# Linear attention with balanced routing on one core: order of copies, lists and first products where attention ends

## The chip, the cores and the metric

One core of a Trainium2 chip. The metric is the device time of one execution in microseconds (us), the median of three runs. The profiled execution is one more run; all starts and durations below come from it, counted from the start of its span.

## What is computed

The reference has two blocks. The first is a linear attention with decay (RWKV-5): for each of 4 batches and 8 heads a state of 48 x 48 goes through 768 steps. The second routes its output, 3072 tokens of 384 values, to 8 experts of 384 tokens each, greedily by the highest logits.

```python
for t in range(S):
    cur = einsum('bhd,bhe->bhde', u * k[:, :, t], v[:, :, t])
    y[:, :, t] = einsum('bhd,bhde->bhe', r[:, :, t], state + cur)
    state = w * state + einsum('bhd,bhe->bhde', k[:, :, t], v[:, :, t])
x = y.transpose(0, 2, 1, 3).reshape(B * S, H * D)
logits = x @ w_gate                      # 3072 x 8
for idx in argsort(-logits.flatten()):   # highest first
    tok, e = idx // E, idx % E           # skipped if tok is taken or e has its 384
for e in range(E):
    out[mask_e] = relu(x[mask_e] @ w1[e]) @ w2[e]     # 384 -> 1024 -> 384
```

Everything is fp32.

## The kernel before

**Attention** (class `Mild`). The work is cut into 24 units n of 128 tokens, four batches for each of six chunks of the sequence. For a unit, TensorE turns r and k, makes the pairs of r and k (`pairs`, g_ps L504), which VectorE masks into AT (L508); ScalarE writes AT's diagonal (L495) from a sum that GpSimd (rk L442 and L443) and VectorE (dd L448) prepare; `outputs` (L531) accumulates the state's part and AT's part in y_ps (L542), and ScalarE copies it to x (L560). Rows of x are turned (`rows_turned`, x_ps L591), copied (xr L598) and stored to DRAM (L599, issued by SyncE). After each fourth unit the router's logits of a chunk are made: `gate` (lg_ps L571, copy L576) and `logits`, one transpose (lt_ps L581) and one copy into LG (L582). The order of `run` is written out by hand, under a manual schedule: an engine executes its instructions in the order of the calls. In a unit in which a chunk ends (`full`, n = 4, 8, 12, 16, 20), `outputs` with its copy of x comes first and `logits` of the chunk before after it.

**Routing** (class `Assignment`). A search on VectorE raises or lowers thresholds until each expert's tokens are chosen. It uses TensorE for counts (prop against ind, L944; wide against ones_h, L955), running sums (st_ps L1075) and lists (some_ps L1408, list_ps L1426). `early` is a generator that already works while attention still runs, on the first five chunks: it picks one expert, the star, and a first list of 256 of its tokens (e_some_ps L1199, then list_ps). The list `steps` says at which places of attention's units its parts are called: its entries name a unit, counted from the end, and a place in it ("states" lies between the state's products and AT's in `outputs`, "last" after `outputs`, "rows" by the rows of units 20 and 21).

**Experts** (class `Experts`). `gather` (xg L1513) issues one indirect DMA per 128 rows from GpSimd; `load_weights` has SyncE load w1 and w2 (L1506), once the expert's number is known (L1499). `turned` turns 128 rows (xT_ps L1528) and ScalarE copies them to xT (L1529). `hidden` multiplies by w1 (h_ps L1541), 3 products for each of 8 outputs j of 128 features, and ScalarE applies relu (L1543). An fp32 product is two matmul instructions.

The first list is worked off by `Experts.early` (L1697), a generator that yields after every product, so that `go(m)` can put m pieces between the steps of the search: two blocks of 128 rows are turned (e_xT_ps L1705, each block in a PSUM tile of its own) and copied (L1706), then 8 outputs of 3 products of 256 columns (e_h_ps L1711, relu L1714), then the second layer (e_o_ps L1719), copied (L1723) and scattered (L1637). At the end of attention the order is written out by hand: the rows of unit 22 out, both blocks of the first list, the rows of unit 23 out, two products, then the search for the first full expert (expert n = 1 of the loop) with products between its steps. Its rows are gathered and `turned`, with the second search's first steps before and between, and the rest of the first list's products ahead of the first turn. From then on `Experts.run` takes over, with `hidden` of n = 1 first; a scheduler, no longer the order of the calls, places the later searches' instructions by their costs. For n = 1 the variable `late` in `run` is true.

PSUM tiles with the same tag (y_ps, kT_ps, rT_ps, g_ps) share space. y_ps takes two banks of 512 fp32 values.

Of the kernel before, what the change touches and what calls it, by code (L numbers as in the profile page):

```python
# [10 lines left out]
F32 = mybir.dt.float32  # L11
# [4 lines left out]
AF = mybir.ActivationFunctionType  # L16
# [258 lines left out]
class Mild:  # L275
# [252 lines left out]
            else:  # L528
                nc.vector.tensor_mul(S, kv, wc)

    def outputs(self, n, between=None):  # L531
        nc, HP, D, C = self.nc, self.HP, self.D, self.C
        b, c = self.units[n]
        AT, rT = self.live[n]["AT"], self.live[n]["rT"]
        vt, S0 = self.vts[:, n % self.NV], self.states[:, b]
        y_ps = self.ps.tile([128, 2, 512], F32, name="y_ps")
        yv = y_ps[:, :, 0:2 * T].rearrange("p o (i t) -> p o i t", t=T)
        seen = set()

        def add(h, lhsT, rhs, stop):  # L540
            o, q = h // 2, h % 2
            nc.tensor.matmul(yv[q * PD:(q + 1) * PD, o // 2, o % 2, :], lhsT, rhs, start=(o // 2, q) not in seen,  # L542
                             stop=stop, skip_group_check=True)
            seen.add((o // 2, q))

        if c > 0:
            for i in range(HP // 2):
                for a in (i, i + HP // 2):
                    for z in range(2):
                        rows = slice(z * PD, z * PD + D)  # L550
                        add(self.head(a, z), S0[rows, a, :], rT[rows, a, :], False)
        if c > 0:
            self.keep(n)
        if between is not None:
            between()
        for a in range(HP):
            for z in range(2):
                add(self.head(a, z), vt[:, self.head(a, z), :], AT[:, z, a, :], True)
        xT = self.xpool.tile([128, HP, T], F32, name=f"x{n % 5}")
        nc.scalar.copy(xT.rearrange("p (o i) t -> p o i t", i=2), yv)  # L560
        self.xts[n] = xT
        del self.live[n]
# [18 lines left out]
        nc.tensor.transpose(lt_ps, lg, self.ident)  # L581
        nc.scalar.copy(self.LG[:, c * B:(c + 1) * B, :], lt_ps.rearrange("p (b e) -> p b e", b=B)[:, :, 0:self.E])  # L582

    def rows_turned(self, ns, tag):
        nc, HP = self.nc, self.HP
        shape = [128, len(ns), HP, T]
        ps = (self.walk.ps if tag == "few" else self.ps).tile(shape, F32, name="x_ps", tag=tag)
        P = PD + self.D
        for i, n in enumerate(ns):
            for o in range(HP):  # L590
                nc.tensor.transpose(ps[:, i, o, 0:P], self.xts[n][0:P, o, :], self.ident[0:P, 0:P])  # L591
        return ps

    def rows_out(self, ns, ps):
# [18 lines left out]
    def run(self, step):  # L613
# [38 lines left out]
        for n in range(N):  # L652
# [47 lines left out]
                if n + 2 < N:  # L700
                    self.diagonal(n + 2, halves[1])
            if n == N - 1:
                self.rows((N - 4, N - 3), "g_ps")
                step(n, "rows")
            self.outputs(n, lambda: step(n, "states"))
            if split:
                self.diagonal(n + 2, halves[1])
            if full:
                self.logits(n // B - 1)
            if n == N - 4:  # L710
                self.own_sum(N - 1)
            step(n, "last")
# [736 lines left out]
def rwkv5_eagle_then_base_layer_balanced(  # L1449
# [12 lines left out]
    nc = tc.nc  # L1462
# [21 lines left out]
    class Experts:  # L1484
# [48 lines left out]
            *_, xT = self.turned(ahead, lambda c: self.ps_t.tile([128, KD, 128], F32, name="xT_ps"))  # L1533
            return xT

        def hidden(self, w1, xT, m, half, progress):
            hid = self.h.tile([128, KF, CAP], F32, name="hid")
            for j in range(KF):
                h_ps = self.ps_h.tile([128, CAP], F32, name="h_ps")
                for f in range(KD):  # L1540
                    nc.tensor.matmul(h_ps[:, 0:m], w1[:, f, ts(j, 128)], xT[:, f, 0:m],  # L1541
                                     start=(f == 0), stop=(f == KD - 1))
                nc.scalar.activation(hid[:, j, 0:m], h_ps[:, 0:m], AF.Relu)  # L1543
                if j == KF // 2 - 1:
                    half(hid)
                progress((j + 1) / KF)
            return hid

        BLOCKS = dict(h0=(0, 0), h1=(0, 1), h2=(1, 0), h3=(1, 1), h4=(2, 0), h5=(2, 1))
# [102 lines left out]
        def run(self, ahead, later, rows, pulls={}, xT=None):  # L1652
            xT, lead = xT or self.turn(ahead), True
            while ahead:
# [28 lines left out]
                def at_product(part):  # L1683
                    progress(1 + part)

                hid = self.hidden(w1, xT, nb * 128, half if whole else lambda hid: None, progress)
                if whole:
                    self.sums_of(left, self.HID_SUMS if many else self.SEVEN_LATE)
                    (self.fifteen if many else self.seven)(left, right, tok, rows, at_product)
# [7 lines left out]
        def early(self, ps, pool, w1, w2, xg, tok, rows, have):  # L1697
            NE = tok.shape[1]
            m = NE * 128
            xT = self.turns[0].tile([128, KD, CAP], F32, name="xT")  # L1700
            hid = pool.tile([128, KF, m], F32, name="e_hid")
            for c in range(NE):
                xT_ps = ps.tile([128, KD, 128], F32, name="e_xT_ps", tag=("y_ps", "rT_ps")[c % 2])
                for f in range(KD):
                    nc.tensor.transpose(xT_ps[:, f, :], xg[:, c, ts(f, 128)], ident)  # L1705
                nc.scalar.copy(xT[:, :, ts(c, 128)], xT_ps)  # L1706
                yield
            for j in range(KF):
                h_ps = ps.tile([128, m], F32, name="e_h_ps", tag=("kT_ps", "rT_ps")[j % 2])
                for f in range(KD):  # L1710
                    nc.tensor.matmul(h_ps, w1[:, f, ts(j, 128)], xT[:, f, 0:m], start=(f == 0), stop=(f == KD - 1))  # L1711
                    if f < KD - 1:
                        yield
                nc.scalar.activation(hid[:, j, :], h_ps, AF.Relu)  # L1714
                yield
            for c in range(NE):
                o_ps = ps.tile([128, DX], F32, name="e_o_ps", tag=("y_ps", "g_ps")[c % 2])
                for j in range(KF):
                    nc.tensor.matmul(o_ps, hid[:, j, ts(c, 128)], w2[:, j, :], start=(j == 0), stop=(j == KF - 1))  # L1719
                    if j < KF - 1:  # L1720
                        yield
                o_sb = pool.tile([128, DX], F32, name="e_o_sb", bufs=2)
                nc.scalar.copy(o_sb, o_ps)  # L1723
                self.scatter(o_sb, have["to"][:, c:c + 1], next(rows))
                yield

    with ExitStack() as whole:
# [6 lines left out]
        with ExitStack() as part:  # L1734
# [7 lines left out]
            def on_tokens(tok):  # L1742
# [2 lines left out]
            early = walk.early(on_star, on_tokens)  # L1745
            U = mild.N
            steps = [(U - 7, "first"), (U - 7, "paired"), (U - 6, "paired"), (U - 5, "products"), (U - 5, "paired"),
                     (U - 3, "turning"), (U - 3, "turning"), (U - 3, "paired"), (U - 2, "last"),
                     (U - 1, "rows"), (U - 1, "last")]

            def step(n, at):
# [3 lines left out]
            with tc.manual_schedule():  # L1755
# [4 lines left out]
                def go(m):  # L1760
                    for _ in range(m):
                        next(pieces, None)

                mild.rows_out((U - 2,), one)
                go(NE)
                mild.rows_out((U - 1,), last)
                go(2)
                search = walk.likely_steps(**first, on_fmax=lambda fmax: have.update(v=x.load_weights(1, fmax)))
                for m in (2, 5, 2, 5, 2, 6, 5):
                    next(search)  # L1770
                    go(m)
                next(search, None)
# [10 lines left out]
                ahead = 1, xg, to, *have["v"]  # L1783
                turned = x.turned(ahead, lambda c: mild.ps.tile([128, KD, 128], F32, name="xT_ps",
                                                                tag=("kT_ps", "rT_ps")[c % 2]))
                go(8)
                next(search)
                go(2)
                next(search)
                for m in (0, 0, 99):  # L1790
                    go(m)
                    xT = next(turned)
                walk.book(first, first=True)
# [86 lines left out]
```

## Time and profile before

| | |
|---|---|
| median of 3 runs | 398.09 us (398.03 to 398.3) |
| profiled execution | 397.39 us |
| its span | 395.7 us |
| instructions | 8692, of them 3243 matmuls |
| attention's last output copied (unit 23) | about 125.3 us from the span's start |
| first product of the first list | 129.6 us |
| first product of the first full expert | 155.09 us |

The span runs from the first to the last instruction that the profile records; 1.7 us of the execution lie outside it. A row of the timeline has the start, the busy time, the engine, the line, the operation, output and inputs by name, sizes, and in brackets the engine's idle time just before with what ended it. PE is TensorE's matmuls, PEld its weight loads, DVE is VectorE, ACT is ScalarE, POOL is GpSimd and SP is SyncE. A row may merge several instructions (x and their number).

### The profile page before, as it was taken

How to read it: one execution, taken by the hardware profiler on the slowest of the kernel's cores; microseconds unless marked ns; L12 is line 12 of the kernel's file. 1: busy time of each engine (PE TensorE's matmuls, PEld its weight loads, DVE VectorE, ACT ScalarE, POOL GpSimd, SP SyncE). 2: the span in 40 equal slices, each digit the busy share in tenths (PEclk: the TensorE clock that was granted, in tenths of full speed). 3: DMA queues.
4: the chain of work that ended last, by engine and by line, in shares of the span. 5: the costliest groups of instructions: out<-in, count | busy, mean ns of one | idle time of the engine just before them, and what ended most of it. 6: DMA issues, size and time to landing. Idle time of an engine off the chain costs nothing. (4 is left out here: it accounts for less than half of the span.)

```text
span 395.7 us, 8692 instructions
## 1 busy us (share of the span) xinstructions
PE 381.1 (96%) x3243; PEld 289.3 (73%) x3243; DVE 266.9 (67%) x934; ACT 162.0 (41%) x429; POOL 138.4 (35%) x173
## 2 busy tenths in 40 slices
PE   7899999999999999999999999999999999999993
PEld 5678888888877765587578569558757856966991
DVE  6755777576885677897839819979578663952630
ACT  4998888888873312222222122121222222222130
POOL 7888877666732013032121120302303211040020
PEclk9999999999999999999999999999999999999998
DMA  9999999898692155371460650109209173380010
GB/s 120 156 183 200 200 173 205 156 169 157 117 342 81 42 200 217 96 282 42 160 239 16 214 210 2 60 0 333 87 21 354 59 275 131 92 308 2 2 61 27
DMA packets 95331, 57.29 MB, mean 145 GB/s; under 512 B 77232, under 2 KB 89520, under 8 KB 95280
## 3 DMA queue, kind: packets, MB, share of 16 engines
q1 hardware_dynamic: 91936, 47.21, 47.7%
q0 software_dynamic: 3104, 9.44, 6.8%
q8 instruction: 27, 0.44, 0.5%
q14 instruction: 24, 0.20, 0.2%
q10 hardware_dynamic: 240, 0.00, 0.0%
HBM read 47.20 MB, written 9.44 MB: 143 GB/s over the span
## 5 line engine op out<-in xcount | busy, mean ns | idle before, releaser
L1541 PE MATMUL h_ps<-xT,w 128*128 128x384 f32 (+1 forms) x384 | 120.7, 467 | 0.6 <-ACT xT L1529 0.6
L1541 PEld LDWEIGHTS h_ps<-xT,w 128*128 128x128 f32 x384 | 66.4, 190 | 38.1 <-issue 2.5
L1543 ACT ACTIVATE hid<-h_ps 128x384 f32<-128x384 f32 (+1 forms) x64 | 29.7, 465 | 91.1 <-PE h_ps L1541 85.1
L495 ACT ACTIVATE AT<-ident,dd 128x128 f32<-128x128 f32 x192 | 59.6, 391 | 1.9 <-DVE dd L448 1.8
L1513 POOL DMA_INDIRECT xg<-x_rows,tok x22 | 22.4, 1017 | 95.6 <-PE h_ps L1541 32.1
L1637 POOL DMA_INDIRECT out_dram<-o_all,to x16 | 17.9, 1120 | 94.6 <-DVE o_all L1625 62.2
L508 DVE COPY_PREDICATED AT<-mask,g_ps 128x512 f32<-128x512 uint8 x48 | 32.6, 733 | 12.1 <-PE g_ps L504 10.6
L1620 ACT COPY res<-p_ps 128x384 f32<-128x384 f32 (+2 forms) x28 | 13.3, 474 | 60.5 <-PE p_ps L1616 60.5
L1643 PE MATMUL o_ps<-w,hid 128*128 128x384 f32 x96 | 33.1, 488 | 0.0
L504 PE MATMUL g_ps<-rT,kT 48*128 48x128 f32 x384 | 27.9, 284 | 0.7 <-DVE AT L508 0.6
L436 POOL TENSOR_TENSOR kss<-krs,wk 128x384 f32<-128x384 f32 x24 | 24.3, 1015 | 8.0 <-DVE krs L340 5.5
L504 PEld LDWEIGHTS g_ps<-rT,kT 48*128 48x128 f32 x384 | 23.4, 187 | 4.0 <-PE unread_ps L418 0.5
L542 PE MATMUL y_ps<-AT,vts 128*64 128x128 f32 x384 | 25.7, 276 | 0.0
L443 POOL TENSOR_TENSOR rk<-rk,u_bc 128x384 f32<-128x384 f32 x24 | 24.2, 1007 | 1.9
L442 POOL TENSOR_TENSOR rk<-krs 128x384 f32<-128x384 f32 x24 | 24.5, 1020 | 0.2 <-DMA krs<-in_r_dram 0.2
L1643 PEld LDWEIGHTS o_ps<-w,hid 128*128 128x128 f32 x96 | 17.2, 190 | 9.5 <-issue 0.2
L542 PEld LDWEIGHTS y_ps<-AT,vts 128*64 128x64 f32 x384 | 20.6, 137 | 1.2 <-issue 0.7
L1616 PE MATMUL p_ps<-T,S 128*128 128x192 f32 x120 | 20.9, 328 | 0.0
L1593 DVE TENSOR_TENSOR H<-hid 128x512 f32<-128x512 f32 x12 | 7.9, 686 | 19.1 <-ACT hid L1543 19.1
L1616 PEld LDWEIGHTS p_ps<-T,S 128*128 128x128 f32 x120 | 19.6, 190 | 0.1
L932 DVE TENSOR_TENSOR own<-counts,same 128x64 f32<-128x64 f32 x21 | 4.7, 222 | 21.7 <-PE counts L944 21.6
L1616 PE MATMUL p_ps<-w,hid 128*128 128x192 f32 (+1 forms) x112 | 19.0, 316 | 0.0
(303 smaller groups left out, 694.0 us busy)
## 6 DMA issues: line engine op xcount, KB each, us to landing
w<-in_moe_w_dram SPq DMA_DIRECT2D x18, 1536.0 KB, 10.2
krs<-in_k_dram SPq DMA_DIRECT2D x24, 192.0 KB, 4.0
krs<-in_r_dram SPq DMA_DIRECT2D x24, 192.0 KB, 4.7
vts<-in_v_dram SPq DMA_DIRECT2D x24, 192.0 KB, 4.7
x_rows<-xr SPq DMA_DIRECT2D x24, 192.0 KB, 3.2
xg<-x_rows,tok POOLq DMA_INDIRECT x22, 4.4
out_dram<-o_all,to POOLq DMA_INDIRECT x16, 2.8
out_dram<-o_sb,to POOLq DMA_INDIRECT x5, 3.0
```

The lines of the kernel that those rows point to most:

```text
L436: self.nc.gpsimd.tensor_mul(self.kss[:, n % self.NS].rearrange("p (g h) d -> p g h d", g=2)[:, :, :, 0:D], src, self.wk.rearrange("p (g h) ...
L442: nc.gpsimd.tensor_mul(rk, self.krs[:, n % self.NK, 1, 0:H, 0:D], self.krs[:, n % self.NK, 0, 0:H, 0:D])
L443: nc.gpsimd.tensor_mul(rk, rk, self.u_bc)
L495: nc.scalar.mul(AT[:, z, a, :], self.ident, dd[:, h:h + 1])
L504: nc.tensor.matmul(g_ps[:, z, a, :], kT[rows, a, :], rT[rows, a, :], start=True, stop=True)
L508: nc.vector.copy_predicated(out=AT[:, z], mask=self.mask.unsqueeze(1).to_broadcast([128, HP, T]), data=g_ps[:, z])
L542: nc.tensor.matmul(yv[q * PD:(q + 1) * PD, o // 2, o % 2, :], lhsT, rhs, start=(o // 2, q) not in seen, stop=stop, skip_group_check=True)
L1513: nc.gpsimd.indirect_dma_start(out=xg[:, c, :], out_offset=None, in_=x_dram[0:within, :], in_offset=bass.IndirectOffsetOnAxis(ap=tok[:, c: ...
L1541: nc.tensor.matmul(h_ps[:, 0:m], w1[:, f, ts(j, 128)], xT[:, f, 0:m], start=(f == 0), stop=(f == KD - 1))
L1543: nc.scalar.activation(hid[:, j, 0:m], h_ps[:, 0:m], AF.Relu)
L1616: nc.tensor.matmul(ps[:, q, :], left[a][:, j, :], right[b][:, j, :], start=(j == 0), stop=(j == KF // 2 - 1))
L1643: nc.tensor.matmul(o_ps, hid[:, j, ts(c, 128)], w2[:, j, :], start=(j == 0), stop=(j == KF - 1))
```

## The change

- `outputs` takes a function `last`, called after its matmuls and before x's copy. In a unit in which a chunk ends, `logits` is called there: its transpose stands where it stood on TensorE, and its copy to LG stands ahead of the copy to x on ScalarE.
- The step of `early` that was called after unit 22's `outputs` is called between its state's products and AT's. The one that was called after the rows of units 20 and 21 is called between the turns of 20 and of 21.
- In `Experts.early`, e_xT_ps is one tile of two banks, a bank for each block; both blocks' copies stand ahead of unit 22's copy to xr. The first output's three products are done as 2 x 3 products of 128 columns, block 0's first; the tags of e_h_ps change places.
- One piece instead of two before the search's second step, five after the same. Two pieces fewer go ahead of the first full expert's turns: they stand between the turns, one in each gap.
- `hidden` of the first full expert does its first two outputs together by row blocks of 128 columns: block 0 for both outputs, block 1 for both, block 2 for both, that is 18 products of 128 columns in place of 6 of 384. The relus of both and the calls of `progress` follow.

```diff
--- before.py
+++ after.py
@@ -528,7 +528,7 @@
             else:
                 nc.vector.tensor_mul(S, kv, wc)
 
-    def outputs(self, n, between=None):
+    def outputs(self, n, between=None, last=lambda: None):
         nc, HP, D, C = self.nc, self.HP, self.D, self.C
         b, c = self.units[n]
         AT, rT = self.live[n]["AT"], self.live[n]["rT"]
@@ -556,6 +556,7 @@
         for a in range(HP):
             for z in range(2):
                 add(self.head(a, z), vt[:, self.head(a, z), :], AT[:, z, a, :], True)
+        last()
         xT = self.xpool.tile([128, HP, T], F32, name=f"x{n % 5}")
         nc.scalar.copy(xT.rearrange("p (o i) t -> p o i t", i=2), yv)
         self.xts[n] = xT
@@ -581,7 +582,7 @@
         nc.tensor.transpose(lt_ps, lg, self.ident)
         nc.scalar.copy(self.LG[:, c * B:(c + 1) * B, :], lt_ps.rearrange("p (b e) -> p b e", b=B)[:, :, 0:self.E])
 
-    def rows_turned(self, ns, tag):
+    def rows_turned(self, ns, tag, between=lambda: None):
         nc, HP = self.nc, self.HP
         shape = [128, len(ns), HP, T]
         ps = (self.walk.ps if tag == "few" else self.ps).tile(shape, F32, name="x_ps", tag=tag)
@@ -589,6 +590,8 @@
         for i, n in enumerate(ns):
             for o in range(HP):
                 nc.tensor.transpose(ps[:, i, o, 0:P], self.xts[n][0:P, o, :], self.ident[0:P, 0:P])
+            if i == 0:
+                between()
         return ps
 
     def rows_out(self, ns, ps):
@@ -700,13 +703,11 @@
                 if n + 2 < N:
                     self.diagonal(n + 2, halves[1])
             if n == N - 1:
-                self.rows((N - 4, N - 3), "g_ps")
-                step(n, "rows")
-            self.outputs(n, lambda: step(n, "states"))
+                rows = self.rows_turned((N - 4, N - 3), "g_ps", lambda: step(n, "rows"))
+                self.rows_out((N - 4, N - 3), rows)
+            self.outputs(n, lambda: step(n, "states"), (lambda: self.logits(n // B - 1)) if full else (lambda: None))
             if split:
                 self.diagonal(n + 2, halves[1])
-            if full:
-                self.logits(n // B - 1)
             if n == N - 4:
                 self.own_sum(N - 1)
             step(n, "last")
@@ -1533,17 +1534,20 @@
             *_, xT = self.turned(ahead, lambda c: self.ps_t.tile([128, KD, 128], F32, name="xT_ps"))
             return xT
 
-        def hidden(self, w1, xT, m, half, progress):
+        def hidden(self, w1, xT, m, half, progress, lead=False):
             hid = self.h.tile([128, KF, CAP], F32, name="hid")
-            for j in range(KF):
-                h_ps = self.ps_h.tile([128, CAP], F32, name="h_ps")
-                for f in range(KD):
-                    nc.tensor.matmul(h_ps[:, 0:m], w1[:, f, ts(j, 128)], xT[:, f, 0:m],
-                                     start=(f == 0), stop=(f == KD - 1))
-                nc.scalar.activation(hid[:, j, 0:m], h_ps[:, 0:m], AF.Relu)
-                if j == KF // 2 - 1:
-                    half(hid)
-                progress((j + 1) / KF)
+            for js in [range(2) if lead else range(1), *([j] for j in range(2 if lead else 1, KF))]:
+                h_ps = {j: self.ps_h.tile([128, CAP], F32, name="h_ps") for j in js}
+                for at in [slice(c * 128, c * 128 + 128) for c in range(m // 128)] if len(js) > 1 else [slice(0, m)]:
+                    for j in js:
+                        for f in range(KD):
+                            nc.tensor.matmul(h_ps[j][:, at], w1[:, f, ts(j, 128)], xT[:, f, at],
+                                             start=(f == 0), stop=(f == KD - 1))
+                for j in js:
+                    nc.scalar.activation(hid[:, j, 0:m], h_ps[j][:, 0:m], AF.Relu)
+                    if j == KF // 2 - 1:
+                        half(hid)
+                    progress((j + 1) / KF)
             return hid
 
         BLOCKS = dict(h0=(0, 0), h1=(0, 1), h2=(1, 0), h3=(1, 1), h4=(2, 0), h5=(2, 1))
@@ -1683,7 +1687,7 @@
                 def at_product(part):
                     progress(1 + part)
 
-                hid = self.hidden(w1, xT, nb * 128, half if whole else lambda hid: None, progress)
+                hid = self.hidden(w1, xT, nb * 128, half if whole else lambda hid: None, progress, late)
                 if whole:
                     self.sums_of(left, self.HID_SUMS if many else self.SEVEN_LATE)
                     (self.fifteen if many else self.seven)(left, right, tok, rows, at_product)
@@ -1699,18 +1703,22 @@
             m = NE * 128
             xT = self.turns[0].tile([128, KD, CAP], F32, name="xT")
             hid = pool.tile([128, KF, m], F32, name="e_hid")
+            xT_ps = ps.tile([128, NE, 512], F32, name="e_xT_ps", tag="y_ps")[:, :, 0:DX].rearrange(
+                "p c (f t) -> p c f t", t=128)
             for c in range(NE):
-                xT_ps = ps.tile([128, KD, 128], F32, name="e_xT_ps", tag=("y_ps", "rT_ps")[c % 2])
                 for f in range(KD):
-                    nc.tensor.transpose(xT_ps[:, f, :], xg[:, c, ts(f, 128)], ident)
-                nc.scalar.copy(xT[:, :, ts(c, 128)], xT_ps)
+                    nc.tensor.transpose(xT_ps[:, c, f, :], xg[:, c, ts(f, 128)], ident)
+                nc.scalar.copy(xT[:, :, ts(c, 128)], xT_ps[:, c])
                 yield
             for j in range(KF):
-                h_ps = ps.tile([128, m], F32, name="e_h_ps", tag=("kT_ps", "rT_ps")[j % 2])
-                for f in range(KD):
-                    nc.tensor.matmul(h_ps, w1[:, f, ts(j, 128)], xT[:, f, 0:m], start=(f == 0), stop=(f == KD - 1))
-                    if f < KD - 1:
-                        yield
+                h_ps = ps.tile([128, m], F32, name="e_h_ps", tag=("rT_ps", "kT_ps")[j % 2])
+                parts = [slice(c * 128, c * 128 + 128) for c in range(NE)] if j == 0 else [slice(0, m)]
+                for n, at in enumerate(parts):
+                    for f in range(KD):
+                        nc.tensor.matmul(h_ps[:, at], w1[:, f, ts(j, 128)], xT[:, f, at],
+                                         start=(f == 0), stop=(f == KD - 1))
+                        if f < KD - 1 and n == 0:
+                            yield
                 nc.scalar.activation(hid[:, j, :], h_ps, AF.Relu)
                 yield
             for c in range(NE):
@@ -1745,7 +1753,7 @@
             early = walk.early(on_star, on_tokens)
             U = mild.N
             steps = [(U - 7, "first"), (U - 7, "paired"), (U - 6, "paired"), (U - 5, "products"), (U - 5, "paired"),
-                     (U - 3, "turning"), (U - 3, "turning"), (U - 3, "paired"), (U - 2, "last"),
+                     (U - 3, "turning"), (U - 3, "turning"), (U - 3, "paired"), (U - 2, "states"),
                      (U - 1, "rows"), (U - 1, "last")]
 
             def step(n, at):
@@ -1761,12 +1769,12 @@
                     for _ in range(m):
                         next(pieces, None)
 
+                go(NE)
                 mild.rows_out((U - 2,), one)
-                go(NE)
                 mild.rows_out((U - 1,), last)
                 go(2)
                 search = walk.likely_steps(**first, on_fmax=lambda fmax: have.update(v=x.load_weights(1, fmax)))
-                for m in (2, 5, 2, 5, 2, 6, 5):
+                for m in (1, 5, 2, 5, 2, 6, 5):
                     next(search)
                     go(m)
                 next(search, None)
@@ -1783,11 +1791,11 @@
                 ahead = 1, xg, to, *have["v"]
                 turned = x.turned(ahead, lambda c: mild.ps.tile([128, KD, 128], F32, name="xT_ps",
                                                                 tag=("kT_ps", "rT_ps")[c % 2]))
-                go(8)
+                go(7)
                 next(search)
                 go(2)
                 next(search)
-                for m in (0, 0, 99):
+                for m in (0, 1, 99):
                     go(m)
                     xT = next(turned)
                 walk.book(first, first=True)
```

## The prediction

> **What bounds the kernel now.** I read the page's first part, then the stretches of busy time by stage, then the timeline of one stage.
>
> ```profile
> PE 381.1 (96%) x3243; PEld 289.3 (73%) x3243; DVE 266.9 (67%) x934; ACT 162.0 (41%) x429; POOL 138.4 (35%) x173
> ```
>
> TensorE is the bound: all that another engine does counts only where TensorE stands still for it. The stretches (columns: window, length, PE, PEld, DVE, ACT, POOL busy, clock, DMA share, GB/s) show where:
>
> ```profile
> 128.00:130.00 2.00, 1.19 (x8) 0.69 (x7) 1.25 (x4) 1.76 (x5) 0.00 (x0) 1.00 0.26 98
> 130.00:150.00 20.00, 19.96 (x94) 13.93 (x93) 15.05 (x71) 3.55 (x9) 2.83 (x3) 1.00 0.41 143
> 150.00:154.00 4.00, 3.72 (x19) 1.97 (x17) 3.57 (x20) 0.96 (x2) 1.65 (x3) 1.00 0.85 324
> 154.00:158.00 4.00, 3.43 (x15) 2.00 (x16) 2.03 (x9) 1.42 (x3) 0.37 (x1) 1.00 0.13 49
> 165.00:385.00 220.00, 219.77 (x1141) 161.33 (x1140) 149.97 (x560) 51.76 (x112) 42.52 (x40) 1.00 0.38 137
> ```
>
> TensorE is short of work at 128 to 130, at the end of attention (ScalarE busy 1.76 of 2), and at 150 to 158, where the first full expert begins. From 165 to 385 it idles 0.2 of 220 us, so what is gained ahead of 165 reaches the end undiminished. The timeline (start, busy time; in brackets the idle time before and what ended it) names the waits:
>
> ```profile
> 115.47 0.25 PE L1199 MATMUL e_some_ps<-e_vals,e_row 128*128 128x32 f16 x4 [0.55 <-ACT LG L582]
> 128.03 0.48 ACT L598 COPY xr<-x_ps 128x384 f32<-128x384 f32 x1
> 128.48 0.55 PE L1705 MATMUL e_xT_ps<-ident,xg 128*128 128x128 f32 x3 [0.24 <-DMA xg<-x_rows,e_tok]
> 129.60 1.13 PE L1711 MATMUL e_h_ps<-xT,w 128*128 128x256 f32 x4 [0.57 <-ACT xT L1706]
> 153.43 1.09 PE L1528 MATMUL xT_ps<-ident,xg 128*128 128x128 f32 x6 [0.26 <-DMA xg<-x_rows,tok]
> 155.09 0.91 PE L1541 MATMUL h_ps<-xT,w 128*128 128x384 f32 x2 [0.57 <-ACT xT L1529]
> 378.11 5.52 PE L1541 MATMUL h_ps<-xT,w 128*128 128x128 f32 x48
> ```
>
> A first product waits twice for the copy of the last turned block (0.57 each), the turns wait for gathered rows (0.24, 0.26), and the early search waits for the logits' copy behind x's (0.55). The last line, from the final expert, gives the price of a narrow product: 48 in 5.52 us. An fp32 product is two such instructions; spaced by their starts they are 0.112 apart at 128 columns, 0.216 at 256 and 0.3225 at 384.
>
> **What the Trainium skill says.** (1) "TensorE: Matmul & The Clock Gate", section "Back-to-back issue gap": the spacing in a stream is set by weight load and matmul together, pipelined. A load takes 190 ns here, yet the narrow row above runs at 0.112: agrees, loads overlap. (2) "ScalarE: Activation LUTs", "What ACT_TABLE_LOAD costs": 186 ns + 0.833 ns an element; 32, 384 and 512 elements give 0.21, 0.51, 0.61, the trace 0.18 to 0.19, 0.48, 0.59. Agrees; the trace's are used. (3) "DMA: Bandwidth & Descriptors", "SWDGE vs HWDGE vs iDMA": each DMA engine takes turns between GpSimd's queue and the hardware's. So gathers share with weight loads: landings take 3.3 to 3.5 us at 124, but 6.0, 5.6 and 4.8 for the second list, issued while the weights stream (agrees). (4) "PSUM — Partial Sum Buffer", "PSUM bank collisions raise a hardware error": two engines are to be kept apart by bank. With a tile of two banks TensorE could write one while ScalarE reads the other; whether it does depends on the wait that the program sets.
>
> **The change part by part** (starts of instructions, before to after).
>
> *Logits' copy ahead of x's, units 4, 8, 12, 16.* Counted from the logits' transpose: it ends at 0.33, x's copy ran 0.12 to 0.71, and the next x_ps transposes came at 1.04. Now the copy of 0.19 waits for the transpose (0.37), x's runs 0.44 to 1.03 (copies overlap by 0.1), and the transposes start at 1.03 + 0.05 for the semaphore: +0.04 each, **+0.16** for four. Bounds 0 (not the last to arrive) and +0.25.
>
> *The same at unit 20.* LG comes 0.46 earlier, so the wait of 0.55 at e_some_ps goes. But its chain runs on through VectorE, where the reduction at L448 waits for GpSimd's rk (115.252), and all following operations stand behind it up to e_acc (117.214), which the second following TensorE step (117.272) awaits. The gap moves there: **0**, bounds -0.45 and 0.
>
> *First list between the row turns.* e_some_ps goes ahead of unit 22's last products, list_ps between the turns of units 20 and 21: token numbers 0.32 earlier (gathers from 123.71 to 123.39, second landing from 128.44 to 128.12). An interruption of a product stream cost about 0.17 at the searches' counts; here one more, **+0.1**, bounds +0.05 and +0.2. It's contained in the times that follow.
>
> *Its rows in one bank pair, first product by blocks.* e_xT_ps becomes a single tile. In the compiled order the second block's transposes then wait for the first block's copy, a **new wait**; behind it stand all products and the search. On ScalarE both xT copies now precede both xr copies. After: LG 128.05 to 128.24; block 0's copy 128.38 to 128.87; block 1's transposes 128.92 (were 128.48); three at 0.11, so first products 129.3 (were 129.60), on block 0 alone; four at 0.112, so counts at 129.75, its VectorE operand being ready at 129.55 (129.45 + 0.1). Counts was at 130.57: 0.82 earlier, with 0.43 of product work still owed: net -0.38. If the new wait weren't one, 0.4 more would be gained until the operand of 129.55 binds, so at most 0.2. The xr stores, later by 0.5 to 1 us, feed only gathers after 145: free.
>
> *The search.* One piece less ahead of it brings the list of the first full expert 1.03 earlier (some_ps, list_ps, gathers: first issue 146.57 to 145.54), its weights' load 0.82 earlier.
>
> *First full expert's turns.* The second search's counts comes at 149.5 (150.97), 0.2 late for its operand; ones_h 150.96 (152.43). Two second products of the early list (4 x 0.3225 = 1.29) are saved to stand between the three turns. Turn 0 waits for its rows: 145.54 + 6.0 = about 151.6, idle 0.6. From there three turns of 0.33, 1.29 of products and 0.1 of joints: 153.98. Before, the last turn ended at 154.33 after waits of 0.14, 0.26 and 0.19. Counts follows at once, as the products between hid both copies; so h_ps may start at 154.15, against 155.085 (+ the 0.17 for the counts that now stands ahead of it, 155.25): **-1.10** up to here.
>
> *Row blocks at its first two outputs.* 36 instructions of 128 columns instead of 12 of 384: 36 x 0.112 - 12 x 0.3225 = **+0.15**; those of the early list, 12 x 0.112 - 6 x 0.216 = +0.04 (together **+0.19**, of which 0.02 lies ahead of the mark above). With only three narrow products after counts, ones_h stands about **+0.35** for VectorE's `wide`. The wait of **-0.13** at st_ps (162.98) goes, the search being ahead. From there the order is the same.
>
> Sum: -1.10 + 0.35 + 0.17 - 0.13 = -0.71; with +0.16 from the four units **-0.55**. Against the profiled execution (397.39, span 395.7, 1.7 outside it): 396.84, span about 395.1. The median of the runs shown is 398.09, 0.7 above that execution: **397.5**.
>
> **Rivals.** *A, the forecast*: 397.5, from -0.2 to -0.9 by its own bounds. *B, rows in time.* The landing of the second list is the largest unknown: bounds 148.9 (3.4 unloaded) and 152.6 (where it was). If it lands by 151.0, the wait of 0.6 goes: -1.15, **396.9**. For it: issued further ahead of the busiest stretch. Against: the weights start earlier as well. *C, rows tied to the weights.* The gathers finish only as the weight stream thins out and land at 152.6 again: +1.0 on turn 0, +0.45 in all, **398.5**. For it: first landing 152.58 beside the weights' end at 153.08; against: the weights are 0.8 earlier too. *D, the other side: narrow products bound by weight loads.* A load is 190 ns and each 128-column instruction needs its own. If 0.19 were the spacing, 48 x (0.19 - 0.112) = +3.8, so **401.3**; from 0.123 it eats the gain, from 0.14 the kernel is over 0.2% slower. Against: 48 of the very same form ran at 0.112 in the last expert. For: here the weights have just been brought in, and searches interrupt the stream.
>
> **How the numbers follow.** Chances: A 0.50, B 0.30, C 0.13, D 0.07. What a measurement of this kernel can tell from no change is about 0.2%, 0.8 us, which the forecast doesn't reach. Faster by more: 0.29 from B, 0.12 from A's far end; slower: D and a hundredth of C, 0.08; the rest, 0.51, within. Range: 396.5 (B with the bounds of unit 20) to 398.6 (C), which leaves out D and the tails, under 0.2.
>
> **What would show it.** Right: second e_xT_ps transposes idle some 0.7, released by ScalarE; counts near 129.75; the second list's gathers issued at 145.5; turn 0 idle 0.6 by DMA, no idle ahead of the first h_ps; narrow ones spaced 0.112; the x_ps after units 4 to 16 late by 0.04. Wrong: a gap between counts and ones_h over 0.5, a landing away from 151.6, a gain at 117, or TensorE idle after 165.

## The result and the profile after

| | before | after |
|---|---|---|
| median of 13 runs | 398.30 us (398.03 to 398.67) | 398.67 us (398.35 to 399.36) |
| ratio | | 1.0012 (95% interval 1.0005 to 1.0020) |
| profiled execution | 397.39 us, span 395.7 us | 398.67 us, span 396.9 us |
| matmuls | 3243 | 3273 |

The kernel became slower by 0.37 us in the median, where 0.55 us less was forecast. The 1.3 us between the two profiled executions mislead: the one of before lies 0.9 us under the median of its kernel. The experiments below were run in four sets, each on one chip; the record numbers these chips 14, 4, 13 and 0. On chips 14 and 0 the kernel before takes 398.2 to 398.3: I call them group A. On chips 4 and 13 it takes 397.3 to 397.4: group B. Which chip gave the table above and the first profile of before isn't on record; by their times the table and the profile after are of A's kind, that profile of before is of B's. Differences of medians below are taken on the same chip only. Profiles are compared on the same chip where there is one of each kernel, and otherwise within a group; x_first, lg_alone and no_blocks, for whose chip there is no profile of before, are set against third_before.

The page's first part, after:

```profile
PE 382.2 (96%) x3273; PEld 291.9 (74%) x3273; DVE 266.5 (67%) x934; ACT 161.5 (41%) x429; POOL 137.8 (35%) x173
```

TensorE is still the bound. The stretches of busy time, with the same columns as before:

```profile
128.00:130.00 2.00, 1.69 (x14) 1.16 (x12) 0.35 (x1) 0.72 (x3) 0.00 (x0) 1.00 0.05 18
130.00:150.00 20.00, 19.71 (x101) 14.38 (x101) 15.64 (x72) 4.99 (x13) 2.51 (x3) 1.00 0.41 143
150.00:154.00 4.00, 3.56 (x17) 1.78 (x16) 3.69 (x20) 0.48 (x1) 1.35 (x2) 1.00 0.97 372
154.00:158.00 4.00, 3.79 (x32) 3.29 (x31) 2.89 (x13) 1.34 (x3) 0.98 (x1) 1.00 0.13 50
165.00:385.00 220.00, 219.67 (x1139) 160.97 (x1138) 149.28 (x555) 51.84 (x113) 41.97 (x40) 1.00 0.38 136
```

The wall-clock windows now hold other work: the last logits' transpose is 1.4 us later than in the profile of before (129.03 against 127.59), the first product of the first full expert 0.3 us. What carries over is the last row: TensorE idles 0.3 of 220 us, so a delay ahead of 165 goes through to the end as a gain would. The waits, in the timeline after:

```profile
115.63 0.25 PE L1200 MATMUL e_some_ps<-e_vals,e_row 128*128 128x32 f16 x4
117.92 0.18 PE L1164 MATMUL e_st_ps<-e_acc,ones 128*128 128x4 bf16 x1 [0.46 <-DVE e_acc L1160]
126.83 0.60 PE L592 MATMUL x_ps<-ident,x 112*128 112x112 f32 x4 [0.32 <-issue]
126.92 0.58 ACT L561 COPY x<-y_ps 128x512 f32<-128x512 f32 x1 [2.29 <-remote]
130.26 0.55 PE L1710 MATMUL e_xT_ps<-ident,xg 128*128 128x128 f32 x3 [0.57 <-ACT xT L1711]
130.64 0.61 PE L1718 MATMUL e_h_ps<-xT,w 128*128 128x128 f32 x4
152.93 0.55 PE L1529 MATMUL xT_ps<-ident,xg 128*128 128x128 f32 x3 [0.40 <-DMA xg<-x_rows,tok]
155.35 0.91 PE L1544 MATMUL h_ps<-xT,w 128*128 128x128 f32 x6
156.48 0.22 PE L956 MATMUL counts<-wide,ones_h 128*128 128x128 f16 x1 [0.21 <-DVE wide L933]
156.53 2.00 PE L1544 MATMUL h_ps<-xT,w 128*128 128x128 f32 x16
378.86 6.00 PE L1544 MATMUL h_ps<-xT,w 128*128 128x128 f32 x48
```

Row by row: e_some_ps has lost its wait of 0.55, and the gap stands at e_st_ps (0.46), as forecast. Before, that step had none:

```profile
117.27 0.18 PE L1163 MATMUL e_st_ps<-e_acc,ones 128*128 128x4 bf16 x1
```

The second block's turn has the new wait on ScalarE (0.57). e_h_ps and h_ps start with no idle time, the first rows of the full expert are waited for (0.40), wide for 0.21, and of the 16 narrow instructions, which take 2.00 in all, most start 0.112 after the one before. New and not forecast is 126.8: TensorE idle at the turn of unit 22, and x's copy of unit 23 on ScalarE beginning 1.84 us after its last product was issued (125.08); "issue" and "remote" say that the trace shows no releaser.

### The profile page after: what moved, and what is told of

Read it like the earlier page. It is cut to its first block, busy times and chain, and to the rows that moved or that the text cites. A ratio compares the mean times of both kernels' runs of the same rounds, so it can differ in the third digit from the quotient of the medians.

```text
span 396.9 us, 8755 instructions
## 1 busy us (share of the span) xinstructions
PE 382.2 (96%) x3273; PEld 291.9 (74%) x3273; DVE 266.5 (67%) x934; ACT 161.5 (41%) x429; POOL 137.8 (35%) x173
## 4 chain that ended last, share of the span: by engine, by line
PE 72%; DVE 8%; ACT 5%; issue 4%; DMA 4%; POOL 3%; another core or an unknown queue 1%; POOLq 0%; ACTq 0%; SPq 0%; DVEq 0%
PE h_ps L1544 26%; PE p_ps L1620 14%; PE o_ps L1647 7%; PE y_ps L542 5%; PE g_ps L504 4%; ACT AT L495 3%; PE e_h_ps L1718 3%; PE x_ps L592 2%; PE kv_ps L521 2%; PE kT_ps L458 2%; PE xT_ps L1529 2%; PE rT_ps L458 2%; DMA xg<-x_rows,tok 2%; DVE W L1597 2%; PE lg_ps L572 1%
## 5 line engine op out<-in xcount | busy, mean ns | idle before, releaser
L1544 PEld LDWEIGHTS h_ps<-xT,w 128*128 128x128 f32 x408 | 68.9, 190 | 37.1 <-issue 2.4
L477 DVE TENSOR_TENSOR rT<-rT_ps,WR 112x512 f32<-112x512 f32 x23 | 15.8, 686 | 4.9 <-PE rT_ps L458 4.9
```

Of the source, the lines that this page charges most:

```text
L1544: nc.tensor.matmul(h_ps[j][:, at], w1[:, f, ts(j, 128)], xT[:, f, at], start=(f == 0), stop=(f == KD - 1))
```

## The experiments

In each, "before" is the kernel before in the same set, on the same chip; times are medians. The ratio is to that, with its 95% interval, which is about 0.3 us to each side: differences of 0.1 to 0.2 us between medians are within it.

**again** (chip 14, A): the changed kernel, no edit.

> The changed kernel once more, for a second profile. Its first profile stands still at two places that the kernel before doesn't: TensorE and ScalarE both late by 0.7 us at 126 (x's copy of unit 23 begins 1.6 us after its last product was issued), and 0.5 us more within the last expert's narrow products at 383. If these belong to the change (theory 1: the program's shape), they return at the same places, +0.7 and +0.5. If they are chance (theory 2), they are gone or elsewhere, and only +0.11 at each of the four x_ps after units 4 to 16 and the gain of 0.9 between 129 and 165 return. Median near 398.7 either way.

Measured: 398.37, before 398.19, ratio 1.0007 (0.9999 to 1.0015). The delay at 126 returned (x's copy 1.77 after the last product, x_ps idle 0.29), so did 0.11 at each of four units. Neither is the chance of one execution.

**x_first** (chip 14, A), the order of the two copies undone:

```diff
-            self.outputs(n, lambda: step(n, "states"), (lambda: self.logits(n // B - 1)) if full else (lambda: None))
+            self.outputs(n, lambda: step(n, "states"))
...
+            if full:
+                self.logits(n // B - 1)
```

> The changed kernel with x's copy ahead of the logits' copy again in the five units, all else as changed. If the order of the two copies is what costs (4 x 0.11 = 0.44 in the trace, less about 0.13 gained at unit 20), this is 0.3 us faster than the changed kernel: about 398.35, and the steps of 0.11 after units 4 to 16 are gone. If the forecast's 0.04 each were right, 0.1 to 0.2 faster only.

Measured: 398.26, ratio 1.0002 (0.9994 to 1.0011), 0.11 below the run of the changed kernel in this set where 0.3 was expected, with intervals too wide to decide. The steps of 0.11 are gone in the profile; the delay at 126 stays.

**lg_alone** (chip 14, A), the reverse: the kernel before with the diff's lines in `outputs` and its call, nothing else.

> The kernel before with one part of the change alone: logits' copy ahead of x's in the five units. If the order costs 4 x 0.11 less 0.13 at unit 20: about +0.3 us, 398.6. By the forecast's price +0.16. If the early list's chain were set by the logits, a gain: below 398.3.

Measured: 398.37, ratio 1.0005 (0.9996 to 1.0013). Against third_before (group A, chip 0) the profile has +0.43 by unit 20 and -0.12 behind it, the +0.3 that was expected; the median shows +0.18 and can't tell it from none.

**no_blocks** (chip 14, A), whole rows in the first full expert:

```diff
-                hid = self.hidden(w1, xT, nb * 128, half if whole else lambda hid: None, progress, late)
+                hid = self.hidden(w1, xT, nb * 128, half if whole else lambda hid: None, progress)
```

> The changed kernel with the first full expert's first outputs by whole rows (6 products of 384 columns in place of 18 of 128); the rest as changed. By the forecast it loses the cover of the last copy (the first product waits 0.5 to 0.6 for the third block) and gets 0.15 back: about 0.4 us slower than the changed kernel, 399.1. If narrow products in this place cost more than they save: at or below the changed kernel's 398.7.

Measured: 398.80, ratio 1.0013 (1.0007 to 1.0020), 0.43 over the changed kernel in the same set, where 0.4 was expected; in the profiles the stretch from the last logits' transpose to the first p_ps is 0.26 longer (43.83 against 43.57 of again). Its timeline has the wait that the row blocks cover:

```profile
155.25 0.25 PE L945 MATMUL counts<-prop,ind 128*128 128x64 bf16 x3
156.03 0.91 PE L1544 MATMUL h_ps<-xT,w 128*128 128x384 f32 x2 [0.54 <-ACT xT L1530]
```

The first product stands behind the third block's copy for 0.54; with row blocks h_ps follows counts at 0.08.

**before_again** (chip 4, B): the kernel before, no edit.

> The kernel before once more, for a second profile, since its first one (397.39) lies 0.9 us under the median of its runs. Five profiles of other kernels share three delays that the first profile of before lacks: 0.3 us by 14 to 33 us, x's copy of unit 23 beginning 1.4 to 1.8 us after its last product was issued (0.33 there), and 0.45 us within the last expert's narrow products. If these are a matter of the execution (theory 2), they are in this profile too, and its span is about 396.6. If the change brings them (theory 1), this profile is as the first, span 395.7, and the change as a whole is to blame.

Measured: 397.48, before 397.32, ratio 1.0004 (0.9996 to 1.0013). The same kernel twice in one set thus differs by 0.16 in the median. Its profile differs from the first one of before by +0.30 at unit 4, -0.28 in the tail and +0.25 behind that, with nothing edited; neither of the two later delays (at 126 and in the last expert) is there. The run left open whether the other chip or the change brings them, since the chip had changed.

**lists_alone** (chip 4, B), the kernel before with the diff's two list steps and `between` in `rows_turned`.

> The kernel before with the two list steps moved (unit 22 between its products, the other between the row turns) and nothing else. The forecast: +0.1 us on TensorE, gathers 0.3 us earlier, which saves the wait of 0.24 for their rows: -0.1 to +0.1. The four profiles with moved lists all show TensorE idle 0.3 to 0.6 before the turn of unit 22 (x_ps at 126.8), which the one without them does not: if the moved lists bring that, this is 0.3 to 0.5 us slower than before, 398.6.

Measured: 397.35, ratio 1.0005 (0.9997 to 1.0013): no difference that can be told. TensorE has +0.06 by unit 23 as forecast. The gathers were issued 0.3 earlier, yet the second landed at 128.91 instead of 128.47 in before_again, so there was a wait for it (0.31) where before_again has none; here an earlier issue was no earlier landing.

**tail_only** (chip 4, B), what is left without these two parts: x_first's edit, and

```diff
-                     (U - 3, "turning"), (U - 3, "turning"), (U - 3, "paired"), (U - 2, "states"),
+                     (U - 3, "turning"), (U - 3, "turning"), (U - 3, "paired"), (U - 2, "last"),
...
-                rows = self.rows_turned((N - 4, N - 3), "g_ps", lambda: step(n, "rows"))
-                self.rows_out((N - 4, N - 3), rows)
+                self.rows((N - 4, N - 3), "g_ps")
+                step(n, "rows")
```

> The changed kernel with the copies' order and the two list steps as before: left are the bank pair, the first list's first product by blocks, the pieces moved between the turns, and the row blocks of the first full expert. By the trace of the changed kernel this part gains 0.9 us between 129 and 165, by the forecast 0.7: 397.4 expected, against 398.2 of before. If the rest of the change doesn't cost what its trace says, and this part gains little, it stays at 398.0 to 398.3.

Measured: 397.10, ratio 0.9996 (0.9988 to 1.0004). The median shows 0.2 of the 0.7 to 0.9 that were expected. The profile, though, stands where the forecast put it: counts at 129.75 (forecast 129.75), the second search's at 149.50 (149.5), turn 0 at 151.58 (151.6), the counts after the turns at 153.91 (153.98). It overstates the gain: the profiled execution (396.62) is the fastest of this kernel's 13 runs.

**tail_apart** (chip 4, B): tail_only, and the second block in another bank as a tile of its own:

```diff
-            xT_ps = ps.tile([128, NE, 512], F32, name="e_xT_ps", tag="y_ps")[:, :, 0:DX].rearrange(
-                "p c (f t) -> p c f t", t=128)
             for c in range(NE):
+                xT_ps = (ps, walk.ps)[c % 2].tile([128, KD, 128], F32, name="e_xT_ps", tag=("y_ps", "few")[c % 2])
```

> The same as the run with the tail alone, but the first list's second block is turned into a tile of its own in another bank, so that its transposes don't wait for the first block's copy (0.5 to 0.7 us of TensorE's idle time in the changed kernel). By the forecast at most 0.2 us faster than the tail alone, because the search's first counts then waits for VectorE instead: 397.2 to 397.4. If the wait on the copy costs its whole length: 396.9.

Measured: 396.85, before 397.32, ratio 0.9990 (0.9982 to 0.9999), 0.25 below tail_only, with intervals that overlap. The timeline of this kernel at the second block:

```profile
128.88 0.52 PE L1711 MATMUL e_xT_ps<-ident,xg 128*128 128x128 f32 x3 [0.49 <-DMA xg<-x_rows,e_tok]
129.24 0.61 PE L1719 MATMUL e_h_ps<-xT,w 128*128 128x128 f32 x4
```

Without the wait on the copy TensorE waits for the rows instead, 0.49 in place of 0.57. In the profiles the tail is 0.18 shorter (43.41 against 43.59), near the forecast's bound of 0.2. The new wait cost little because it lay over another.

**pair_before and pair_after** (chip 13, B): both kernels, no edit, side by side.

> The kernel before, profiled on the same chip as the next run. So far the profiles fall in two groups by the chip: on one, before takes 398.2 and every profile has x's copy of unit 23 begin 1.4 to 1.8 us after its last product and 0.45 us lost in the last expert's narrow products; on the other, before takes 397.3 and no profile has them. If it is the chip, this profile and that of the next run are alike in both places. If the changed kernel brings them, only the next run has them.

> The changed kernel on the same chip. From the parts: four times 0.11 for logits ahead of x, less 0.13 at unit 20, lists +0.1 (up to +0.4 where the rows land late), the tail -0.8. Sum -0.4 to 0.0 against the run before on this chip if the two delays are the chip's and alike in both; +0.2 to +0.4 if the change brings the delay at unit 23 or makes it longer.

Measured: 397.38 and 397.37, the latter with ratio 1.0002 (0.9994 to 1.0011). On this chip the change does nothing that can be measured. Neither profile has the delay at 126; x's copy of unit 23, first before, then after:

```profile
125.00 0.58 ACT L560 COPY x<-y_ps 128x512 f32<-128x512 f32 x1 [0.88 <-PE y_ps L542]
125.28 0.59 ACT L561 COPY x<-y_ps 128x512 f32<-128x512 f32 x1 [0.78 <-PE y_ps L542]
```

**lists_back** (chip 13, B), the changed kernel with tail_only's second diff alone.

> The changed kernel with the two list steps where they stood before. If the moved lists cost 0.1 on TensorE and gain nothing, this is 0.1 us faster than the changed kernel; if they also bring TensorE's idle time before the turn of unit 22 (0.3 to 0.6 in their company on one chip), 0.4 to 0.7 faster; if their earlier rows were of use, slower by up to 0.2.

Measured: 397.21, ratio 0.9995 (0.9986 to 1.0003), 0.16 below pair_after, which the intervals don't tell from none.

**best** (chip 13, B), tail_apart with the logits' copy ahead of x's at unit 20 alone (`if n == N - 4`).

> The tail of the change with the second block in a tile of its own, and logits' copy ahead of x's at unit 20 alone, lists as before. The parts: -0.8 from the tail, up to -0.1 from the tile of its own, -0.13 from unit 20: 0.5 to 1.0 us faster than before on the same chip. If unit 20's 0.13 is not real, the same as the run with the tail and its own tile (0.1% faster than before).

Measured: 396.93, before 397.38, ratio 0.9991 (0.9982 to 0.9999). By its ratio no better than tail_apart; at unit 20, where -0.13 was hoped for, its profile shows +0.01, no gain.

**third_before, third_lists_back, third_after** (chip 0, A), the kernel before, lists_back and the changed kernel once more, which settle what B couldn't.

> The kernel before, for a profile on the chip on which it takes 398.2, if this is that chip. If the chip alone is late at unit 23, x's copy there begins over 1 us after its last product in this profile too. If it begins after 0.33 as on the other chip, the change brings the delay on that chip. On the other chip: 397.4, nothing new.

> The changed kernel with the two list steps where they were. On the chip with 398.2: if the moved lists bring TensorE's idle time of 0.3 to 0.6 before the turn of unit 22, it is gone here and the time 0.4 us below the changed kernel's, at 398.1; if not, 0.1 below. On the other chip 397.2 once more.

> The changed kernel beside these two. On the chip with 398.2: 0.2 to 0.4 us over before and idle time at 126 again. On the other chip: within 0.2 us of before, no idle time there.

Measured: 398.29 (ratio 0.9997, 0.9988 to 1.0005), 398.30 (0.9997, 0.9989 to 1.0005) and 398.58 (1.0006, 0.9998 to 1.0014). The timelines at the end of attention, in this order:

```profile
125.91 0.60 PE L591 MATMUL x_ps<-ident,x 112*128 112x112 f32 x4
126.14 0.58 ACT L560 COPY x<-y_ps 128x512 f32<-128x512 f32 x1 [1.99 <-PE y_ps L542]
```

```profile
126.24 0.60 PE L592 MATMUL x_ps<-ident,x 112*128 112x112 f32 x4
126.49 0.59 ACT L561 COPY x<-y_ps 128x512 f32<-128x512 f32 x1 [2.00 <-PE y_ps L542]
```

```profile
126.78 0.54 PE L592 MATMUL x_ps<-ident,x 112*128 112x112 f32 x4 [0.32 <-issue]
126.86 0.59 ACT L561 COPY x<-y_ps 128x512 f32<-128x512 f32 x1 [2.27 <-remote]
```

The kernel before has the late copy on this chip too, 1.45 after its last product. So the chip, and not the change, brings it. With the lists back it is 1.46; with the lists moved it is 1.82, and only then does TensorE stand idle at x_ps. The runs third_lists_back and third_after differ by the lists alone and share the chip, so on it the longer delay is the lists' doing (0.28 in the medians). In group B all nine copies there, the first profile's among them, come at 0.33.

## Why the prediction was wrong

The same stretches of TensorE's work, each against a profile of the kernel before. The profile of third_after is set against third_before, pair_after against pair_before and tail_only against before_again, each from the same chip; after and again are set against third_before too, of their group but not, as far as is known, of their chip. Each number is the change in the time between two marks, in us:

| from mark to mark | forecast | after (A) | again (A) | third_after (A) | pair_after (B) | tail_only (B) |
|---|---|---|---|---|---|---|
| start to logits' transpose, unit 4 | 0 | 0.00 | -0.04 | -0.03 | -0.08 | -0.17 |
| to that of unit 20: four full units | +0.16 | +0.44 | +0.44 | +0.42 | +0.43 | -0.01 |
| to e_st_ps: unit 20 | 0 | -0.13 | -0.11 | -0.12 | -0.14 | -0.01 |
| to the last y_ps: the lists on TensorE | +0.10 | +0.08 | +0.07 | +0.07 | +0.07 | +0.01 |
| to the last logits' transpose | 0 | +0.39 | +0.32 | +0.38 | 0.00 | 0.00 |
| to the first p_ps of the first full expert: the tail | -0.81 | -0.44 | -0.48 | -0.28 | -0.43 | -0.61 |
| to the end | 0 | -0.04 | -0.20 | -0.18 | -0.14 | -0.24 |
| sum | -0.55 | +0.30 | 0.00 | +0.26 | -0.29 | -1.04 |

(-0.81 is the -0.71 of the forecast without the +0.1 of the lists, which it contained. The first row and "to the end" have no edit in them: they show how far single executions differ, and the sums contain it.) Three terms were of the wrong size, by 0.2 to 0.5 each: the price of the new wait at the four full units, the gain of the tail, and the cost of the moved lists (this one in group A alone). A fourth fault lies under them: the forecast took its waits from one profile and carried them over to the medians by adding 0.7, but that profile is of B's kind and the medians of A's, so the place where the third term failed could not be seen in it.

**"+0.04 each".** It was 0.11, in both groups, in every run that has this part (for four units lg_alone has +0.43, lists_back +0.44; x_first, without it, +0.01). Unit 8 before:

```profile
55.65 0.33 PE L581 MATMUL lt_ps<-ident,lg 128*128 128x128 f32 x1
55.77 0.59 ACT L560 COPY x<-y_ps 128x512 f32<-128x512 f32 x1 [0.63 <-PE y_ps L542]
56.58 0.44 PEld L591 LDWEIGHTS x_ps<-ident,x 112*128 112x128 f32 x4
56.69 0.55 PE L591 MATMUL x_ps<-ident,x 112*128 112x112 f32 x4
57.17 0.38 PE L504 MATMUL g_ps<-rT,kT 48*128 48x128 f32 x2
```

and after:

```profile
56.09 0.33 PE L582 MATMUL lt_ps<-ident,lg 128*128 128x128 f32 x1
56.54 0.59 ACT L561 COPY x<-y_ps 128x512 f32<-128x512 f32 x1
57.18 0.39 PEld L592 LDWEIGHTS x_ps<-ident,x 112*128 112x128 f32 x4
57.19 0.60 PE L592 MATMUL x_ps<-ident,x 112*128 112x112 f32 x4
57.72 0.38 PE L504 MATMUL g_ps<-rT,kT 48*128 48x128 f32 x2
```

From lt_ps, x_ps went from 1.04 to 1.10: +0.06, the forecast's step (0.04) and nearly its size. But g_ps went from 1.52 to 1.63, +0.11. The four transposes themselves take 0.05 longer (0.60 for 0.55). In the trace's records the first weight load before lies 0.11 ahead of its matmul (56.58, 56.69) and the next matmul follows at 0.10; after, load and matmul start together (57.18, 57.19) and the next follows at 0.15. In this place the load itself waits: it starts 0.14 after the end of the load ahead of it, while in the old kernel it followed at once. So I read the other 0.05 as the price of starting again, with the overlap of load and product lost once more. That it is the load that matters can be seen at the turn of unit 22 in third_after. There TensorE stood idle for 0.32 too, but the first load had gone ahead:

```profile
126.39 0.14 PEld L592 LDWEIGHTS x_ps<-ident,x 112*128 112x128 f32 x1 [0.20 <-issue]
126.79 0.33 PEld L592 LDWEIGHTS x_ps<-ident,x 112*128 112x128 f32 x3 [0.25 <-issue]
```

Its second product follows at 0.095 and the four take 0.54. In after and again, where the load starts with the product in this place, the second follows at 0.15 and the four take 0.60. The forecast priced the wait at the full units and left out the restart.

**"-1.10 ... -0.71".** The tail lasts, from the last logits' transpose to p_ps, 43.62 (after), 43.78 (third_after) and 43.67 (pair_after); the forecast's 44.48 - 0.81 = 43.67 is among them, and tail_only met four of its marks within 0.1. What failed was the other end of the difference: 44.48 is the first profile of before alone. Three further profiles of before took 44.05 (chip 0), 44.09 (chip 13) and 44.20 (chip 4); two runs with the same code in this stretch took 43.90 (lg_alone) and 44.58 (lists_alone, whose second block came late). That first execution waited 0.24 for the first list's second block. In before_again TensorE doesn't stand still there, and both blocks are one row:

```profile
128.05 1.01 PE L1705 MATMUL e_xT_ps<-ident,xg 128*128 128x128 f32 x6
```

The first execution also took 0.2 longer than pair_before and third_before, though not than before_again, from the first e_h_ps to the first h_ps. The forecast counted waits for gathered rows as if they were fixed. Against before on the same chip the gain is 0.28 (chip 0), 0.43 (chip 13) and 0.61 (chip 4), not 0.81.

**"The gathers 0.32 earlier ... +0.1".** On TensorE this was right (+0.07). But in group A the moved lists also cost 0.32 to 0.39 between the last y_ps and the last logits' transpose: all five profiles with moved lists there have it (x_first +0.33 and no_blocks +0.34 besides the three of the table), the two with the steps in place do not (third_lists_back +0.01, lg_alone -0.05). On B it is 0.00 in each. This part made the change a loss on A: there the lists' +0.3 to +0.4 is the size of the tail's gain, and without it third_lists_back takes 398.30 against 398.32 of before. Why ScalarE's copy of unit 23 is late in that group, and why moving two small TensorE steps 2 us ahead of it lengthens the lateness from 1.45 to 1.82, isn't settled; no transfer, instruction fetch or engine shows in the trace as its releaser. In every profile of both groups an instruction fetch of 16 KB begins 1.3 to 1.5 us before the last y_ps product and is over before that product starts, so its place doesn't tell the groups apart. lists_alone wasn't run on A.

Right were: the gap that moves from e_some_ps to e_st_ps with no gain of its own at unit 20 (best: +0.01). The -0.12 in the table isn't a gain of the copy: TensorE came 0.4 late to unit 20, GpSimd, which sets this stretch, only 0.3 (in pair_after rk ends 0.98 after the logits' transpose in place of 1.10), so a part of the delay was absorbed. Right too were the new wait on ScalarE (0.57 for some 0.7) with little lost by it, the narrow products of the first full expert at 0.112 apart from those next to a search's step (so rival D fell), the flight of 6.0 for the second list (issued 146.88, first turn 152.93: the landing moved with the issue, against B's hope and C's fear), and row blocks worth about 0.4 (0.43 in the medians, 0.26 in the tails of two profiles).

The sum of the rows with an edit then: +0.43 - 0.12 + 0.07 - 0.43 = -0.05 on B (pair_after), where the medians say -0.01; with +0.36 more on A, +0.3, where they say +0.37, +0.18 and +0.26. That rival C's 398.5 lies nearest to the measured 398.67 is luck: its cause, rows landing at the old time, didn't occur. D, the other rival with this sign, had the wrong mechanism too.

Small slips of the forecast's arithmetic don't matter to this: 48 x (0.19 - 0.112) is 3.7, not 3.8, and the two prices of narrow products are 0.16 and 0.05, not 0.15 and 0.04. Its bounds for A, -0.2 to -0.9, are narrower than those of its terms, which add up to about -0.4 to -1.2.

## What to carry to other kernels

Take a wait that a gain is to come from out of more than one execution: a wait on a transfer that was 0.24 in one profile was nothing in the next, and 0.2 to 0.5 of the 0.81 forecast for the tail rested on one execution's waits. A step that makes the bounding engine wait at a place where it didn't can cost the wait and the restart (here 0.06 + 0.05), in every round of the loop, while a saving at the end comes once: on chip 13 four units' 0.11 ate the whole tail. Before a difference of 0.1% is believed or explained, both kernels have to be profiled on the same chip, and more than once.

## What the runs showed of the hardware

Chips 0 and 13 ran the same program 0.9 us apart at the same granted clock (0.995 both), for the most part at two places: third_before against pair_before is equal to 0.03 until the last y_ps, then 0.34 later at the last logits' transpose (the late copy) and 0.48 more within the last expert's 48 narrow products. The latter is the last row of the timeline after: 6.00 in place of the 5.52 of before, with the same instructions. It lies in three of the 47 spacings, the same three in all eight profiles of group A: 0.36 to 0.40, 0.21 and 0.18 to 0.21 in place of 0.112. All eight profiles of A (chips 14 and 0, and after) have both delays, and none of the nine of B (chips 4 and 13, and the first of before). What differs between the chips isn't shown.
